# Attention scores from raw float32 tiles, with the 64-row tile first

## The chip, the cores and the metric

The kernel runs on one core of a Trainium2 chip, as one program. The core has five engines that each work through their own list of instructions in order: TensorE (PE in the profile, with its weight loads as PEld), VectorE (DVE), ScalarE (ACT), GpSimd (POOL) and SyncE (SP, which here issues every DMA). The metric is the device time of one execution in microseconds (us). Three runs of the kernel before took 1394.97, 1399.61 and 1401.06 us, median 1399.61.

## The reference

Attention with a computed position bias, and then two mixture layers:

```python
scores = scale * np.matmul(q, k.transpose(0, 1, 3, 2))      # 2 batches, 8 heads, 576 rows, 64 wide
x = (psi_rel / psi_i)[..., None]                            # 576 x 576 x 1
h = np.maximum(x @ w1 + b1, 0.0)                            # 32 hidden
bias = h @ w2                                               # one bias for each head, for both batches
scores = scores + bias.transpose(2, 0, 1)[None, :, :, :]
attn = np.exp(scores - np.max(scores, axis=-1, keepdims=True))
attn = attn / (np.sum(attn, axis=-1, keepdims=True) + 1e-09)
out = np.matmul(attn, v)
# then on the 1152 x 512 result: 4 experts (512-1024-512) weighted by given probabilities,
# then 8 experts (512-1024-512) weighted by a gate with 8 rounds of row and column scaling
```

Everything is float32.

## The kernel before

**Stages.** The attention comes first and takes about 200 us; the two mixture layers follow and take the rest. The change touches the attention alone.

**Bias groups.** The bias is made in 36 groups of 16 query rows. For a group DVE or ACT writes four hidden tiles (`emit_hid`), PE multiplies them by w2 in four quarter-height tiles (`emit_bias_mm`, tile `bps`), ACT copies the product out in two pieces into a staging tile (`emit_bias_out`, tile `bsts`), and SP writes that to a table in DRAM (`bd`, one for each row tile t = 0 to 4). The staging tile has three places, so the ACT copy of a group waits until the DMA of the group three before it has landed. A group's product takes a place of tag `sc` when it fills two banks, else the one place of tag `bps`. `load_bias` reads the table back as tile `bt` (two buffers): two DMAs for t < 4, four for t = 4.

**Units.** A unit is one pass over 128 query rows for a pair of heads: for t < 4 (t, head pair p, batch b), for t = 4 (the last 64 rows of both batches together) only (t, p). There are 36 units, numbered k = 0 to 35. `emit_S` computes the scores of both heads (tile `sc`, two places, both taken by one unit), `emit_max` adds the bias and takes the row maximum on DVE (tile `s`), `emit_exp` is ACT, `emit_T` transposes on PE two units later (tile `tp`; the tail and the reciprocals go into the scores' own banks while groups are left), `emit_evac` copies out (tile `at`), `emit_P` multiplies by V (tile `po`, one bank for all) three units later, and `emit_x` scales the product into `rows` on DVE. In each unit of the loop one more bias group is made (`groups(1)`), until all 36 are. From k = 16 to 18 and from 23 on, each unit also does one part of the preparation of the mixture layer (`pieces`, tiles `x10A`, `x10S`): ACT rounds, DVE or POOL subtracts.

**Scores before.** q and k are loaded raw (`qr`, `kr`); `prep_q` and `prep_k` split each into a rounded float32r tile and the float32r rest; `emit_S` adds three float32r products (rest x rounded, rounded x rest, rounded x rounded) in two column halves of 288, each for two heads that sit in the two 64-row halves of the array: 12 matmuls for t < 4, 24 for t = 4, where the zeros in q keep the batches apart.

**Order.** The order of every engine is the order in which the lines are written; nothing reorders it. SP's list too: a DMA that waits for a tile holds back all DMAs behind it.

Of the kernel before, what the change touches and what calls it, by code (L numbers as in the profile page):

```python
# [9 lines left out]
F32 = mybir.dt.float32  # L10
F32R = mybir.dt.float32r
AF = mybir.ActivationFunctionType
ALU = mybir.AluOpType
# [3 lines left out]
B, H, S, D = 2, 8, 576, 64  # L17
# [8 lines left out]
WARM = 10  # L26
# [22 lines left out]
def attn_moe_moe(ctx: ExitStack, tc: tile.TileContext, pack, keep, rel, qT, kT, vT, w, out):  # L49
# [12 lines left out]
    xa = pool("xa")  # L62
# [113 lines left out]
    def attention(moe):  # L176
# [26 lines left out]
        bdram = [dram.tile([H, (128 if t < 4 else 64) + 1, W], F32, name=f"bd{t}") for t in range(5)]  # L203


        tps_ = [(t, p) for t in (0, 4, 1, 2, 3) for p in range(4)]
        units = [(t, p, b) for t, p in tps_ for b in range(2 if t < 4 else 1)]
        U = len(units)
        kk, qq, bt, rawk, rawq = {}, {}, {}, {}, {}


        def load_k(p, b):
            i = 2 * p + b
            r = xa.tile([128, 1280], F32, tag=f"x0{XA[i % 4]}", name=f"kr{p}{b}")[:, 0:S]
            for h in range(2):
                sy.dma_start(out=r[64 * h:64 * h + 64], in_=kT[p, b, 0:64, S * h:S * h + S])
            rawk[p, b] = r

        def prep_k(p, b, hi):
            r = rawk.pop((p, b))  # L220
            kk[p, b] = ata.tile([128, 2, S], F32R, name=f"kk{p}{b}")
            h = kk[p, b][:, 0, :]
            if hi is sc:
                sc.activation(out=h, in_=r, func=AF.Copy)
            else:
                ve.tensor_copy(h, r)
            ve.tensor_tensor(out=kk[p, b][:, 1, :], in0=r, in1=h.bitcast(F32), op=ALU.subtract)

        def load_q(t, p):
            r = ata.tile([128, 256], F32, tag="qraw", name=f"qr{t}{p}", bufs=3)  # L230
            for h in range(2):
                sy.dma_start(
                    out=r[64 * h:64 * h + 64].rearrange("p (b c) -> p b c", b=2),
                    in_=qT[t, p, 0:64].rearrange("p (b h c) -> p h b c", b=2, h=2)[:, h],
                )
            rawq[t, p] = r

        def prep_q(t, p):
            r = rawq.pop((t, p))
            a = ata.tile([128, 2, 256], F32R, tag="qq", name=f"qq{t}{p}", bufs=3)  # L240
            ve.tensor_copy(a[:, 0, :], r)
            ve.tensor_tensor(out=a[:, 1, :], in0=r, in1=a[:, 0, :].bitcast(F32), op=ALU.subtract)
            qq[t, p] = a

        def load_bias(t, p):

# [21 lines left out]

        free = [(i, hids_[:, i * S:i * S + S]) for i in range(6)]
        taken = {}  # L270
        MORE = 56

        def emit_hid(g, eng, q):
            tt = 4 * g + q
# [62 lines left out]
        def emit_S(u):  # L337
            t, p, b = units[u]
            o = [ps.tile([128, 2, 512], F32, tag="sc", name=f"sc{u}{h}", bufs=2) for h in range(2)]

            todo = [(x, y, bb) for x, y in ((0, 1), (1, 0), (0, 0)) for bb in ([b] if t < 4 else [0, 1])]
            for j in range(2):
                for i, (x, y, bb) in enumerate(todo):
                    for h in range(2):
                        d = slice(64 * h, 64 * h + 64)
                        pe.matmul(  # L346
                            out=o[h][:, j, 0:288],
                            lhsT=qq[t, p][d, x, 128 * bb:128 * bb + 128],
                            rhs=kk[p, bb][d, y, 288 * j:288 * j + 288],
                            start=i == 0,  # L350
                            stop=i == len(todo) - 1,
                        )
# [98 lines left out]
        kq = [(p, b) for p in range(4) for b in range(2)]  # L451

        gp.memset(ones, 1.0)
        for _ in range(WARM):
            pe.matmul(out=po_all[:, 0, 0:128], lhsT=ones, rhs=ones, start=True, stop=True)
# [6 lines left out]
        load_q(*tps_[1])  # L462
        load_k(*kq[2])
        ve.tensor_scalar(b1psi, cst[:, C_PSI:C_PSI + 144], b1col, None, op0=ALU.mult)
        ve.tensor_scalar(w2n, cst[:, C_W2:C_W2 + 32], 8.0, None, op0=ALU.mult)
        ve.tensor_scalar(T, T, w1col, None, op0=ALU.mult)

        NGR = S // 16
        order = list(range(8)) + list(range(32, NGR)) + list(range(8, 32))
        made = 0  # L470
        started = 0

        def hids(k, engs=()):
            nonlocal started
            for i in range(k):
                if started < 4 * NGR and (free or started == 6):
                    emit_hid(order[started // 4], sc if i in engs else ve, started % 4)
                    started += 1
# [6 lines left out]
                    emit_bias_out(g, emit_bias_mm(g))  # L485
                    made += 1

        FIRST = 8
        hids(8, (1, 5))
        for g in range(FIRST):  # L490
            groups(1)
            if g == 0:
                prep_q(*tps_[0])
            if g == 1:
                prep_k(*kq[0], ve)
            hids(4, (1,))
            if g == 3:
                load_k(*kq[3])
            if g == 4:
                prep_k(*kq[1], ve)  # L500
            if g == 6:
                load_k(*kq[4])
                load_q(*tps_[2])

        load_bias(*tps_[0])
        load_bias(*tps_[1])
        load_k(*kq[5])
        load_q(*tps_[3])
        prep_q(*tps_[1])
        prep_k(*kq[2], sc)  # L510
        for _ in range(3):
            groups(1)
            hids(4)
        prep_k(*kq[3], sc)

        ti, work, first_split = 0, [], None
        for k in range(U + 3):
            first = False
            if k < U:
                t, p, b = units[k]  # L520
                first = b == 0
                if first:
                    ti = tps_.index((t, p))
                emit_S(k)
                emit_max(k)
                if k > 0:
                    emit_recip2(k - 1)
                if k >= 4:
                    emit_x(k - 4)
            elif k == U:  # L530
                emit_recip2(k - 1)
                emit_x(k - 4)
                st_sc.close()
                st_a.close()
                moe.open1()
                first_layer = moe.L1(0)
                for fn in first_layer[0:3]:
                    fn()
# [6 lines left out]
                emit_exp(k, 1)  # L545
            if k >= 2 and k - 2 < U:
                emit_evac(k - 2, 2, sc)
            groups(1)
            if k >= 2 and k - 2 < U:
                emit_evac(k - 2, 1, sc if made < NGR else ve)  # L550
            hids(2)
            if k < U:
                emit_recip(k)
            hids(2)
            if k >= 3 and k - 3 < U:
                emit_P(k - 3)
                if k >= U:
# [10 lines left out]
            if k < 4:  # L568
                prep_k(*kq[k + 4], sc)
# [409 lines left out]
```

## Time and profile before

The profiled execution took 1395.53 us; its span from the first to the last instruction is 1393.6 us, so 1.9 us lie around it. Its mean granted TensorE clock is 0.989.

| stretch (us) | what | PE busy | DVE busy | ACT busy | granted clock | DMA share |
|---|---|---|---|---|---|---|
| 0 to 26.26 | first bias groups | 21.21 | 21.33 | 18.62 | 1.00 | 0.66 |
| 26.26 to 56.03 | units 0 to 4 | 21.25 | 19.42 | 17.77 | 0.77 | 0.80 |
| 56.03 to 110.84 | units 5 to 15 | 51.53 | 38.98 | 41.74 | 1.00 | 0.69 |
| 110.84 to 149.03 | units 16 to 23 | 35.97 | 30.53 | 31.73 | 1.00 | 0.53 |
| 149.03 to 201.24 | units 24 to 35 | 43.46 | 40.65 | 38.99 | 1.00 | 0.40 |
| 201.24 to 1393.60 | mixture layers | 1170.51 | 651.80 | 357.81 | 0.99 | 0.13 |

A stretch starts where PE starts the scores of a unit. Busy time of PE is the union of matmuls that overlap, with modelled ends, so PE can be busy and not at its peak. A granted clock of 1.00 is 2.4 GHz and 0.50 is 1.2 GHz.

### The profile page before, as it was taken

The numbers are of one execution on the slowest core, as the hardware profiler recorded it, in microseconds if no ns is written. First come the engines' busy times: TensorE is split into PE (matmuls) and PEld (weight loads), VectorE is DVE, ScalarE is ACT, GpSimd is POOL, SyncE is SP. The second block draws the span as 40 slices with busy tenths as digits, with TensorE's granted clock in tenths as the row PEclk, the third lists the DMA queues.
The fourth block names the chain that finished last, engine by engine and source line by source line (L and its number), as shares of the span: only waits on it lengthen the run. The fifth ranks groups of instructions, "written<-read, shape, count | busy, mean of one in ns | idle before, by whom it ended". The sixth has DMA issues, their size and how long they took to land.

```text
span 1393.6 us, 22438 instructions
## 1 busy us (share of the span) xinstructions
PE 1343.9 (96%) x8763; PEld 1171.4 (84%) x8763; DVE 802.7 (58%) x1786; ACT 506.7 (36%) x1208; POOL 389.3 (28%) x391
## 2 busy tenths in 40 slices
PE   7899888999999999999989999999999999999998
PEld 3676677899898898888878898898998988988987
DVE  7768778464473563575584473564554644736543
ACT  6768764232241241343232241331331422413311
POOL 0111234053061260242151160250440622603400
PEclk9899999999999999999999999999999999999999
DMA  7765521011020020021021020020110200301110
GB/s 210 196 176 151 148 66 61 31 61 61 1 91 32 31 91 1 10 66 47 5 87 31 1 91 31 31 91 1 62 61 1 92 31 16 99 9 32 60 39 31
DMA packets 42169, 84.67 MB, mean 61 GB/s; under 512 B 10320, under 2 KB 17744, under 8 KB 42064
## 3 DMA queue, kind: packets, MB, share of 16 engines
q1 hardware_dynamic: 42064, 83.24, 19.7%
q8 instruction: 69, 1.13, 0.3%
q14 instruction: 36, 0.29, 0.1%
HBM read 69.97 MB, written 13.25 MB: 60 GB/s over the span
## 4 chain that ended last, share of the span: by engine, by line
PE 83%; DVE 9%; ACT 3%; DMA 2%; issue 1%; SPq 1%; DVEq 0%; ACTq 0%
PE y L726 41%; PE B L647 16%; PE C L647 10%; PE A L647 10%; DVE s L364 2%; PE po L435 2%; PE sc L346 1%; ACT s L377 1%; DMA bt<-bd 1%; PE bps L297 1%; PE tp L409 1%; ACT bsts L326 1%; DMA bd<-bsts 1%; DVE wt L157 0%; ACT at L418 0%
## 5 line engine op out<-in xcount | busy, mean ns | idle before, releaser
L726 PE MATMUL y<-gb,h 128*128 128x512 f32 x2592 | 717.8, 397 | 0.0
L726 PEld LDWEIGHTS y<-gb,h 128*128 128x128 f32 x2592 | 454.1, 189 | 57.2 <-issue 0.2
L162 POOL TENSOR_TENSOR gb<-rawb,gb 128x512 fp32r<-128x512 f32 x94 | 126.6, 1359 | 637.1 <-ACT gb L161 605.4
L658 ACT ACTIVATE h<-c 128x320 fp32r<-128x320 f32 (+1 forms) x288 | 119.2, 439 | 402.7 <-DVE c L655 401.5
L655 DVE TENSOR_TENSOR u<-B,s 128x320 f32<-128x320 f32 (+1 forms) x192 | 87.7, 457 | 307.9 <-PE B L647 307.9
L661 DVE SCALAR_TENSOR_TENSOR h<-c,h 128x320 fp32r<-128x320 f32 (+1 forms) x288 | 165.7, 592 | 49.1 <-ACT h L658 43.8
L655 DVE TENSOR_TENSOR c<-C,u 128x320 f32<-128x320 f32 (+1 forms) x192 | 87.6, 456 | 61.3 <-PE C L647 57.9
L162 POOL TENSOR_TENSOR ga<-rawa,ga 128x512 fp32r<-128x512 f32 x94 | 120.4, 1300 | 4.5 <-ACT ga L161 4.5
L162 POOL TENSOR_TENSOR ga<-wt,ga 128x512 fp32r<-128x512 f32 x94 | 104.6, 1132 | 47.7 <-ACT ga L161 27.5
L669 ACT ACTIVATE s<-A 128x320 f32<-128x320 f32 (+1 forms) x96 | 39.5, 411 | 181.3 <-PE A L647 181.2
L658 ACT ACTIVATE h<-A 128x320 fp32r<-128x320 f32 (+1 forms) x96 | 39.1, 408 | 151.0 <-PE A L647 150.5
L655 DVE TENSOR_TENSOR c<-B,s 128x320 f32<-128x320 f32 (+1 forms) x96 | 43.9, 458 | 81.6 <-PE B L647 80.3
L161 ACT ACTIVATE gb<-rawb 128x512 fp32r<-128x512 f32 x96 | 60.0, 626 | 67.6 <-DMA rawb<-in_w 67.6
L377 ACT ACTIVATE s<-s,stat 128x576 f32<-128x576 f32 x72 | 55.4, 769 | 41.5 <-DVE stat L364 40.7
L435 PEld LDWEIGHTS po<-at,V 128*64 128x64 f32 x800 | 39.4, 137 | 33.9 <-DVE rows L445 32.0
L647 PE MATMUL C<-x20S,ga 128*128 128x320 f32 x384 | 67.4, 311 | 0.0
L647 PE MATMUL A<-x20A,ga 128*128 128x320 f32 x384 | 67.1, 310 | 0.0
L647 PEld LDWEIGHTS C<-x20S,ga 128*128 128x128 f32 x384 | 62.1, 190 | 5.8
L647 PEld LDWEIGHTS A<-x20A,ga 128*128 128x128 f32 x384 | 62.0, 190 | 5.7
L647 PE MATMUL B<-x20S,ga 128*128 128x320 f32 x384 | 66.5, 308 | 0.0
L647 PEld LDWEIGHTS B<-x20S,ga 128*128 128x128 f32 x384 | 61.4, 188 | 5.7
L435 PE MATMUL po<-at,V 128*64 128x128 f32 (+1 forms) x800 | 47.7, 267 | 15.6 <-DVE rows L445 15.4
(163 smaller groups left out, 1917.0 us busy)
## 6 DMA issues: line engine op xcount, KB each, us to landing
rawa<-in_w SPq DMA_DIRECT2D x48, 512.0 KB, 4.0
rawb<-in_w SPq DMA_DIRECT2D x48, 512.0 KB, 4.9
bd<-bsts SPq DMA_DIRECT2D x36, 295.5 KB, 3.4
bt<-bd SPq DMA_DIRECT2D x16, 512.0 KB, 4.5
qr<-in_qT SPq DMA_DIRECT2D x40, 64.0 KB, 2.9
kr<-in_kT SPq DMA_DIRECT2D x16, 144.0 KB, 3.1
V<-in_vT SPq DMA_DIRECT2D x4, 512.0 KB, 4.6
bt<-bd SPq DMA_DIRECT2D x8, 256.0 KB, 4.1
```

The lines of the kernel that those rows point to most:

```text
L161: sc.activation(out=z(0), in_=src, func=AF.Copy)
L162: lo.tensor_tensor(out=z(1), in0=src, in1=z(0).bitcast(F32), op=ALU.subtract)
L297: pe.matmul(out=o[32 * q:32 * q + 32, j, 0:n], lhsT=w2n, rhs=hid[g, q][:, n * j:n * j + n], start=True, stop=True,)
L364: ve.tensor_tensor_reduce(out=s.rearrange("p (a j) -> p a j", a=2), in0=scps.pop((u, h))[:, :, 0:288], in1=bt[t, p][:, S * h:S * h + S].re ...
L377: sc.activation(out=s, in_=s, func=AF.Exp, scale=-1.0, bias=stat[u][:, h:h + 1], accum_out=stat[u][:, 2 + h:3 + h],)
L435: pe.matmul(out=o[64 * h:64 * h + 64, c0:c0 + n], lhsT=V[p][:, j, col:col + D], rhs=rhs, start=j == 0, stop=j == 4,)
L647: pe.matmul(out=ban[o], lhsT=a, rhs=x[:, z, k, :], start=not more and i == 0, stop=i == 5, skip_group_check=more,)
L655: ve.tensor_tensor(out=t[o], in0=ban[a], in1=t[b], op=ALU.add)
L658: sc.activation(out=h[f][:, 0, half, :], in_=src, func=AF.Relu)
L661: ve.scalar_tensor_tensor(out=h[f][:, 1, half, :], in0=src, scalar=0.0, in1=h[f][:, 0, half, :].bitcast(F32), op0=ALU.max, op1=ALU.subtract,)
L669: sc.activation(out=t["s1"], in_=ban["A"], func=AF.Copy)
L726: pe.matmul(out=self.y[t], lhsT=a, rhs=x, start=g == 0 and f == 0 and i == 0, stop=g == NP - 1 and f == 1 and i == 2,)
```

## The change

Four edits, all in the attention.

1. `emit_S` multiplies raw q by raw k as plain float32, one product in place of three: 4 matmuls for t < 4. For t = 4 each batch becomes a tile of 64 columns of the array, so 8 matmuls of 64 rows by 64 columns. `prep_q`, `prep_k` and the split tiles go; k is loaded straight into its tile, q into one of four buffers.
2. The order of the row tiles becomes 4, 0, 1, 2, 3 and that of the bias groups 32 to 35, then 0 to 31. Nine groups come before the loop in place of eleven; unit 4 makes two. In the first four units each unit now starts a new head pair, and k, V, q and the bias for the following ones are loaded in these units.
3. `emit_x(k - 4)` stands before `emit_S(k)` and `emit_max(k)` in place of behind them.
4. Six plain float32 matmuls of ones (`busy(6)`) follow the scores of units 0, 1 and 2.

```diff
-        tps_ = [(t, p) for t in (0, 4, 1, 2, 3) for p in range(4)]
+        tps_ = [(t, p) for t in (4, 0, 1, 2, 3) for p in range(4)]
...
         def load_k(p, b):
...
+            kk[p, b] = ata.tile([128, S], F32, name=f"kk{p}{b}")
             for h in range(2):
-                sy.dma_start(out=r[64 * h:64 * h + 64], in_=kT[p, b, 0:64, S * h:S * h + S])
-            rawk[p, b] = r
-
-        def prep_k(p, b, hi):
...
+                sy.dma_start(out=kk[p, b][64 * h:64 * h + 64], in_=kT[p, b, 0:64, S * h:S * h + S])
...
-        MORE = 56
+        MORE = 76
...
-            todo = [(x, y, bb) for x, y in ((0, 1), (1, 0), (0, 0)) for bb in ([b] if t < 4 else [0, 1])]
+            n = 128 if t < 4 else 64
             for j in range(2):
-                for i, (x, y, bb) in enumerate(todo):
+                for bb in [b] if t < 4 else [0, 1]:
+                    i = 0 if t < 4 else 64 * bb
                     for h in range(2):
                         d = slice(64 * h, 64 * h + 64)
                         pe.matmul(
-                            out=o[h][:, j, 0:288],
-                            lhsT=qq[t, p][d, x, 128 * bb:128 * bb + 128],
-                            rhs=kk[p, bb][d, y, 288 * j:288 * j + 288],
-                            start=i == 0,
-                            stop=i == len(todo) - 1,
+                            out=o[h][i:i + n, j, 0:288],
+                            lhsT=qq[t, p][d, 128 * bb + i:128 * bb + i + n],
+                            rhs=kk[p, bb][d, 288 * j:288 * j + 288],
+                            start=True,
+                            stop=True,
                         )
...
-        order = list(range(8)) + list(range(32, NGR)) + list(range(8, 32))
+        order = list(range(32, NGR)) + list(range(32))
...
-        FIRST = 8
+        FIRST = 4
...
+        load_q(*tps_[1])
+        load_k(*kq[2])
+        load_k(*kq[3])
         load_bias(*tps_[0])
         load_bias(*tps_[1])
...
+        load_v(0)
+        for g in range(5):
             groups(1)
-            hids(4)
+            hids(4, (1,))
...
+                if k >= 4:
+                    emit_x(k - 4)
                 emit_S(k)
+                if k < 3:
+                    busy(6)
                 emit_max(k)
                 if k > 0:
                     emit_recip2(k - 1)
-                if k >= 4:
-                    emit_x(k - 4)
...
-            groups(1)
+            groups(2 if k == 4 else 1)
...
             if first:
                 if ti + 2 < len(tps_):
-                    prep_q(*tps_[ti + 2])
-                if ti + 4 < len(tps_):
-                    load_q(*tps_[ti + 4])
+                    load_q(*tps_[ti + 2])
...
             if k < 2:
-                load_k(*kq[k + 6])
-            if k < 8 and k % 2 == 0:
-                load_v(k // 2)
+                load_k(*kq[2 * k + 4])
+                load_k(*kq[2 * k + 5])
+            if k < 3:
+                load_v(k + 1)
```

SP, the DMAs ahead of the first units; before (kr and qr are raw k and q, bd the table in DRAM, bt the bias read back, the digits are row tile or head pair):

```order
L216 DMA kr10_137<-in_kT 64x576 x2
L329 DMA bd0_104<-bsts_110 16x8x591 x4
L216 DMA kr11_224<-in_kT 64x576 x2
L329 DMA bd0_104<-bsts_110 16x8x591 x3
L216 DMA kr20_266<-in_kT 64x576 x2
L232 DMA qr02_269<-in_qT 64x2x128 x2
L329 DMA bd0_104<-bsts_110 16x8x591
L255 DMA bt00_284<-bd0_104 128x2x512
L256 DMA bt00_284<-bd0_104 128x2x64
L255 DMA bt01_287<-bd0_104 128x2x512
L256 DMA bt01_287<-bd0_104 128x2x64
```

SP, the same place in the changed kernel (kk is k, V0 the values of head pair 0):

```order
L215 DMA kk11_218<-in_kT 64x576 x2
L235 DMA bt40_221<-bd4_108 64x2x512
L236 DMA bt40_221<-bd4_108 64x2x64
L235 DMA bt40_221<-bd4_108 64x2x512
L236 DMA bt40_221<-bd4_108 64x2x64
L235 DMA bt41_226<-bd4_108 64x2x512
L236 DMA bt41_226<-bd4_108 64x2x64
L235 DMA bt41_226<-bd4_108 64x2x512
L236 DMA bt41_226<-bd4_108 64x2x64
L197 DMA V0_100<-in_vT 128x4x256
L201 DMA V0_100<-in_vT 64x2x64 x2
L309 DMA bd0_104<-bsts_110 16x8x591 x6
```

Six writes of groups to DRAM now stand behind the eight bias reads and the three DMAs of V.

DVE, a unit in the middle of the attention, before (s and stat are the maximum, rows is emit_x, hids the next group's hidden tiles):

```order
L364 ISA s6_748,stat6_747<-sc60_731,bt03_580 128x576
L364 ISA stat6_747 128x1
L364 ISA s6_748,stat6_747<-sc61_732,bt03_580 128x576
L364 ISA stat6_747 128x1
L387 RECIPROCAL stat5_677<-stat5_677 128x2
L445 TENSOR_TENSOR rows0_76<-po_95,at22_624 128x128
L283 TENSOR_SCALAR hids_109<-T_99,b1psi_98 128x352 x2
```

DVE, a unit of the changed kernel:

```order
L426 TENSOR_TENSOR rows0_76<-po_95,at42_744 128x128
L345 ISA s8_854,stat8_853<-sc80_845,bt02_711 128x576
L345 ISA stat8_853 128x1
L345 ISA s8_854,stat8_853<-sc81_846,bt02_711 128x576
L345 ISA stat8_853 128x1
L368 RECIPROCAL stat7_793<-stat7_793 128x2
L263 TENSOR_SCALAR hids_109<-T_99,b1psi_98 128x320 x4
```

The product of unit k - 4 is read ahead of the maximum of unit k, in place of behind it and its reciprocal.

## Rows read from the trace of the kernel before

**Rows 1.** Timeline of PE, scores of units and the first mixture matmul (start, duration).
```profile
26.26 1.05 PE L346 MATMUL sc<-kk,qq 64*128 64x288 f32 x11 [0.81 <-ACT bsts L326]
...
56.03 1.34 PE L346 MATMUL sc<-kk,qq 64*128 64x288 f32 x12
...
69.14 1.93 PE L346 MATMUL sc<-kk,qq 64*128 64x288 f32 x24
...
97.78 1.27 PE L346 MATMUL sc<-kk,qq 64*128 64x288 f32 x12
...
106.53 1.13 PE L346 MATMUL sc<-kk,qq 64*128 64x288 f32 x12
...
110.84 1.14 PE L346 MATMUL sc<-kk,qq 64*128 64x288 f32 x12
...
149.03 1.06 PE L346 MATMUL sc<-kk,qq 64*128 64x288 f32 x12
...
201.24 1.15 PE L647 MATMUL A<-x10A,ga 128*128 128x320 f32 x6
```

**Rows 2.** Waits of DVE at 50 to 150 us (total us, times, longest).
```profile
DVE s L364 <- DMA bt<-bd: 7.0, 3, 2.7
```

**Rows 3.** Waits of PE at 150 to 200 us.
```profile
PE po L435 <- DVE rows L445: 8.7, 11, 1.5
```

**Rows 4.** Stretch of the half clock (length, busy PE, PEld, DVE, ACT, POOL, clock, DMA).
```profile
28.86:39.10 10.24, 6.86 (x42) 3.33 (x44) 6.82 (x20) 4.99 (x12) 1.42 (x4) 0.50 0.72 206
```

**Rows 5.** Timeline of PE, plain float32 bias products of two widths.
```profile
89.42 0.72 PE L297 MATMUL bps<-hids,w2n 128*32 128x304 f32 x8
...
151.26 1.07 PE L297 MATMUL bps<-hids,w2n 128*32 128x512 f32 x8
```

**Rows 6.** Timeline of SP, issues (start, time on SP's queue).
```profile
8.77 5.59 SPq L329 DMA_DIRECT2D bd<-bsts  x4
14.41 1.24 SPq L216 DMA_DIRECT2D kr<-in_kT  x2
...
20.26 1.23 SPq L232 DMA_DIRECT2D qr<-in_qT  x2
...
24.90 0.39 SPq L255 DMA_DIRECT2D bt<-bd  x1
...
39.17 0.58 SPq L197 DMA_DIRECT2D V<-in_vT  x1
39.85 1.20 SPq L201 DMA_DIRECT2D V<-in_vT  x2
41.15 0.55 SPq L329 DMA_DIRECT2D bd<-bsts  x1
...
62.14 0.60 SPq L255 DMA_DIRECT2D bt<-bd  x1
```

**Rows 7.** Page, DMA issues: KB each, median us from issue to landing.
```profile
bd<-bsts SPq DMA_DIRECT2D x36, 295.5 KB, 3.4
bt<-bd SPq DMA_DIRECT2D x16, 512.0 KB, 4.5
...
kr<-in_kT SPq DMA_DIRECT2D x16, 144.0 KB, 3.1
```

**Rows 8.** Timeline of ACT, first exponential and a group copied out after it.
```profile
29.79 0.78 ACT L377 ACTIVATE s<-s,stat 128x576 f32<-128x576 f32 x1 [3.00 <-DVE stat L364]
...
33.82 1.05 ACT L326 ACTIVATE bsts<-bps,cst 128x16 f32<-128x16 f32 x2 [2.40 <-DMA bd<-bsts]
```

**Rows 9.** Timeline of DVE, a late unit.
```profile
158.97 0.29 DVE L100 TENSOR_TENSOR x10S<-t,x10S 128x128 fp32r<-128x128 f32 x1 [1.16 <-ACT x10S L99]
...
161.04 0.27 DVE L445 TENSOR_TENSOR rows<-po,at 128x128 f32<-128x128 f32 x1
```

**Rows 10.** Groups of DVE by line at 0 to 400 us (busy us, mean ns).
```profile
L242 DVE TENSOR_TENSOR qq<-qr,qq 128x256 fp32r<-128x256 f32 x20 | 8.5, 425 | 0.7
L227 DVE TENSOR_TENSOR kk<-kr,kk 128x576 fp32r<-128x576 f32 x8 | 6.1, 758 | 9.9 <-ACT kk L224 8.1 <-DMA kr<-in_kT 1.7
```

More of the change, by code (lines that the diff above doesn't have):

```diff
@@ L203, in attention @@
         bdram = [dram.tile([H, (128 if t < 4 else 64) + 1, W], F32, name=f"bd{t}") for t in range(5)]
-        tps_ = [(t, p) for t in (0, 4, 1, 2, 3) for p in range(4)]
+        tps_ = [(t, p) for t in (4, 0, 1, 2, 3) for p in range(4)]
         units = [(t, p, b) for t, p in tps_ for b in range(2 if t < 4 else 1)]
         U = len(units)
-        kk, qq, bt, rawk, rawq = {}, {}, {}, {}, {}
+        kk, qq, bt = {}, {}, {}
         def load_k(p, b):
-            i = 2 * p + b
-            r = xa.tile([128, 1280], F32, tag=f"x0{XA[i % 4]}", name=f"kr{p}{b}")[:, 0:S]
+            kk[p, b] = ata.tile([128, S], F32, name=f"kk{p}{b}")
             for h in range(2):
-                sy.dma_start(out=r[64 * h:64 * h + 64], in_=kT[p, b, 0:64, S * h:S * h + S])
-            rawk[p, b] = r
-        def prep_k(p, b, hi):
[L220 to L227, printed above, removed]
+                sy.dma_start(out=kk[p, b][64 * h:64 * h + 64], in_=kT[p, b, 0:64, S * h:S * h + S])
         def load_q(t, p):
-            r = ata.tile([128, 256], F32, tag="qraw", name=f"qr{t}{p}", bufs=3)
+            qq[t, p] = ata.tile([128, 256], F32, tag="qq", name=f"qq{t}{p}", bufs=4)
             for h in range(2):
                 sy.dma_start(
-                    out=r[64 * h:64 * h + 64].rearrange("p (b c) -> p b c", b=2),
+                    out=qq[t, p][64 * h:64 * h + 64].rearrange("p (b c) -> p b c", b=2),
                     in_=qT[t, p, 0:64].rearrange("p (b h c) -> p h b c", b=2, h=2)[:, h],
                 )
[L236 to L243, printed above, removed]
         def load_bias(t, p):
@@ L453, in attention, with busy @@
         gp.memset(ones, 1.0)
-        for _ in range(WARM):
-            pe.matmul(out=po_all[:, 0, 0:128], lhsT=ones, rhs=ones, start=True, stop=True)
+        def busy(n):
+            for _ in range(n):
+                pe.matmul(out=po_all[:, 0, 0:128], lhsT=ones, rhs=ones, start=True, stop=True)
+        busy(WARM)
         sy.dma_start(out=cst, in_=pack)
@@ L461, in attention @@
         sy.dma_start(out=kept, in_=keep)
-        load_q(*tps_[1])
-        load_k(*kq[2])
         ve.tensor_scalar(b1psi, cst[:, C_PSI:C_PSI + 144], b1col, None, op0=ALU.mult)
@@ L491, in attention @@
             groups(1)
[L492 to L495, printed above, removed]
             hids(4, (1,))
[L497 to L503, printed above, removed]
+        load_q(*tps_[1])
+        load_k(*kq[2])
+        load_k(*kq[3])
         load_bias(*tps_[0])
         load_bias(*tps_[1])
[L507 to L511, printed above, removed]
+        load_v(0)
+        for g in range(5):
             groups(1)
-            hids(4)
-        prep_k(*kq[3], sc)
+            hids(4, (1,))
         ti, work, first_split = 0, [], None
@@ L553, in attention @@
                 emit_recip(k)
-            hids(2)
+            hids(6 if k == 3 else 2)
             if k >= 3 and k - 3 < U:
@@ L567, in attention @@
                 load_bias(*tps_[ti + 2])
-            if k < 4:
-                prep_k(*kq[k + 4], sc)
             if k < 2:
-                load_k(*kq[k + 6])
-            if k < 8 and k % 2 == 0:
-                load_v(k // 2)
+                load_k(*kq[2 * k + 4])
+                load_k(*kq[2 * k + 5])
+            if k < 3:
+                load_v(k + 1)
             if k == 8:
```

## The prediction

> **What bounds the kernel now.** I read the table of stretches first. The mixture layers, from 201.24 us on, keep PE busy nearly throughout, and no line of theirs changes; what the change is worth must come out of the first 201.24 us. There I went along PE's timeline from one start of scores to the next [rows 1]. Units 5 to 15 take 110.84 - 56.03 = 54.81 us for eleven, 4.98 each, but the dense ones take 110.84 - 106.53 = 4.31. The difference sits in one place: from 69.14 (the first unit of the 64-row tile) to 97.78 five units take 28.64 us, 7.1 more than five dense ones. The waits of DVE name the cause: the maximum waits 7.0 us in three waits for the bias read back [rows 2]. A unit of that tile comes one to a head pair, so its four bias DMAs have half as long to land.
>
> At 150 to 200 us PE waits 8.7 us for `emit_x` [rows 3]: the product's bank is read on DVE behind the maximum, which waits for the scores. In the first 56 us neither PE nor DVE nor ACT is full; there I looked at SP's issues and their landings [rows 6, 7] and at what ACT waits for [rows 8].
>
> **Scores.** No row shows a plain float32 matmul in 64-row halves. The nearest is the bias product, plain float32 in four quarter-height tiles: 304 columns take 0.72 us and 512 take 1.07 [rows 5], so 0.35 / 208 = 1.68 ns a column plus 0.21 fixed. The four run together: in turn each column would cost 0.42 ns, less than in float32r, where six full-height products of 320 columns take 1.15 us at 201.24 [rows 1], 0.49 ns a column without the fixed part. And float32r runs two 64-row halves together: twelve scores matmuls of 288 columns take 1.06 at 149.03 [rows 1], where twelve in turn would take about 2 by those products. If plain float32 in halves overlaps too, a unit's scores are 2 x 288 x 1.68 ns + 0.21 = 1.18 us, 0.12 more than now. If the halves take turns, it is 4 x 0.484 + 0.21 = 2.15, 1.09 more. The best is no fixed part, 0.97, 0.09 less than now. I take 1.18, because both kinds of tiles in the trace overlap. For the 64-row tile four tiles together give 1.18, pairs 2.15, against 1.93 now at 69.14 [rows 1]; these units will wait for loads, so this counts nothing.
>
> The scores stand in the loop that sets a dense unit: scores, half of the maximum, two exponentials with two evacuations, and the next scores need the bank that the last of these frees. PE itself is as full. So 0.12 is paid for each dense unit: 4.43.
>
> **Splits that go.** On DVE 6.1 us for k and 8.5 for the rests of q [rows 10], with their copies. In the dense units DVE waits for PE's scores anyway, so I count nothing; in the first units their cover is ACT and SP, which stay late.
>
> **The start.** SP issues in order. From its rows [rows 6]: a k tile 1.25 us, q 1.25, V 1.9 with gaps, a group's write 0.6, one bias DMA 0.39 to 0.60, so four with gaps 1.7 to 2.6; I take 2.2. The fourth group left SP at 8.77 + 5.59 = 14.4; without the splits between them on DVE I put it at 13.6. Then SP holds q, two k tiles, eight bias reads and V: 13.6 + 1.25 + 2.5 + 4.4 + 1.9 = 23.65. Only then comes the write of the fifth group. It lands 3.4 us after issue at the median [rows 7]; with the bias and V bytes ahead of it I take 3.8: 27.45. The eighth group needs that group's staging place, as ACT does now at 33.82, where it waits 2.40 us for such a landing [rows 8]. Its copy takes 1.05: 28.5. The first scores need the banks that this copy frees, so they start at 28.5 against 26.26, although two groups fewer come first.
>
> By then PE has had nothing for some 9 us; in the trace a stretch of gaps like this stands at the half clock, 1.2 GHz, for 10.24 us [rows 4]. So the first scores take 2.2 (the 0.97 doubled, and the fixed part), the first half of the maximum 0.9, two exponentials 0.78 each [rows 8]: 33.2. Six fill matmuls of 128 columns are 6 x 0.215 = 1.3 us at full clock and 2.6 at half. They stand ahead of the tenth group's product, which leaves ACT at about 35.3. Now SP: its write, q, four bias reads, two k tiles end at 35.3 + 0.6 + 1.25 + 2.2 + 2.5 = 41.85, and k lands 3.1 after its last issue [rows 7] at 44.4: unit 2. V, a write, q, four reads, two k tiles: 41.85 + 1.9 + 0.6 + 1.25 + 2.2 + 2.5 = 50.3, landed 52.8: unit 3. V and a write at 52.2; the bias of unit 4 needs that write landed (55.6) and then 4.5 us [rows 7]: 60.1. From the maximum to the next scores a dense unit takes 4.31 - 1.06 = 3.25, so unit 5 starts at 63.4, against 56.03: **+7.4**. The fills don't change this: between them PE waits 6 to 8 us for loads.
>
> Here the Trainium skill speaks the other way ("DMA: Bandwidth & Descriptors", Issuing engines are not separate DMA queues): the sequencer's time to start a DMA "is usually small relative to the DMA itself". By the rows 47 DMAs of about 0.6 us are 28 us of SP in the 37 from 13.6 to 50.3, and a landing is 3 to 4.5; the rule's result is the first rival below.
>
> **The rest.** Units 5 to 15 have no 64-row tile any more, and a bias read has three units to land: 11 x 4.43 = 48.7 in place of 54.81, **-6.1**. Units 16 to 23: five or six dense ones of eight pay 0.12, **+0.7**. In units 24 to 35 two of three run at the pace of a chain that starts at the maximum, goes through ACT's evacuations and rounding and ends in DVE's subtraction (its wait of 1.16 for ACT [rows 9]) ahead of the next maximum. The moved `emit_x`, 0.27 long [rows 9], of which I count 0.2, now stands between that subtraction and the maximum. So the 8.7 us of PE's wait are not a gain: where it goes, this chain is late next, 8 x 0.2 = 1.6 dearer, and only the third without rounding gains some 0.4, 4 x 0.3 with the longer scores: **+0.3**.
>
> Sum: 7.4 - 6.1 + 0.7 + 0.3 = +2.3. On the profiled execution, 1395.53 with 1.9 around its span, that is 1397.8. That execution lies 4.1 below the median of the runs; on the median 1399.61 it is 1402. What waited for the 64-row tile's loads in the middle waits for them at the start. Within 0.5% is 7.0 us, about what a measurement tells from no change.
>
> **Rivals.** *A lean start*: issues cost little and only landings count. Then the first bias read lands at about 22.5, unit 0's scores run at 22, five units at 4.43 to 5 put unit 5 at 44 to 47. -10.5 - 6.1 + 1 gives 1384; half of it, with unit 5 near 52, gives 1391. For it: DMA share is 0.80, not 1, at units 0 to 4. Against: SP's rows, which are the same instructions. Taken at 1386.
> *A longer start*: bias DMAs at 0.60 each (+0.4 a unit's four, four times), landings 0.7 longer, fills at half clock: unit 5 near 68, +7; and the bias of row tiles 1, 2 and 3 is now read in the very unit that makes its last group, so SP waits there for 3.4 us each time. With 1 us lost at each, 1410.
> *Halves in turn* (slower): plain float32 in 64-row halves does not overlap. Each of 32 units pays 1.09 in place of 0.12: 32 x 0.97 = 31, 1433. For it: no row shows the pair; against: both parts of it. It decides from 0.15 us a unit more than I take (scores of 1.33): 32 x 0.15 = 4.7, which with +2.3 is 7.
>
> **Numbers.** My forecast 0.56 (1402, its own range 1393 to 1409), lean start 0.17, longer start 0.17, halves in turn 0.10. Range 1389 to 1412: it leaves out the halves, the lower half of the lean start and the end of the longer one, 0.2 in all. Faster by over 0.5%: 0.16 of the lean start and 0.04 of mine, 0.20. Slower: 0.10 + 0.11 + 0.03 = 0.24. Between: 0.56.
>
> **What would show it.** In the changed profile: unit 0's scores near 28.5, with ACT waiting for a landed write before the eighth group's copy; units 2 and 3 waiting for k; unit 5 at 63; a half clock between 25 and 50; scores rows of 1.18; 4.43 from unit to unit in 5 to 15; PE's wait for `emit_x` gone at 150 to 200 us, and the first mixture matmul at 203 all the same. Unit 5 before 56, or scores of 2.15, would make the prediction wrong.

## The result and the profile after

The changed kernel takes 1412.38 us (median of four runs, 1408.82 to 1413.96) against 1397.92 us for the kernel before in the same runs (four, 1394.97 to 1401.06). The ratio is 1.0100, 95% interval 1.0074 to 1.0125: slower by 1%. The forecast was no change (1402), and the time lies at the very end of the stated range (1389 to 1412). What happened is nearest to the rival called the longer start (1410), for more reasons than that rival named.

The profiled execution took 1413.96 us, span 1412.2. Its timeline of PE, start and duration of a unit's scores in us (compare with [rows 1]):

```profile
31.78 2.19 PE L327 MATMUL sc<-kk,qq 64*64 64x288 f32 x14 [10.99 <-ACT bsts L306]
...
37.98 1.20 PE L327 MATMUL sc<-kk,qq 64*64 64x288 f32 x16
...
47.38 4.51 PE L327 MATMUL sc<-kk,qq 64*64 64x288 f32 x16 [5.73 <-DMA kk<-in_kT]
...
60.03 1.18 PE L327 MATMUL sc<-kk,qq 64*64 64x288 f32 x10 [0.63 <-DMA kk<-in_kT]
...
64.59 1.24 PE L327 MATMUL sc<-kk,qq 64*128 64x288 f32 x8
...
76.85 1.93 PE L327 MATMUL sc<-kk,qq 64*128 64x288 f32 x8
...
82.08 1.27 PE L327 MATMUL sc<-kk,qq 64*128 64x288 f32 x8
...
165.99 1.24 PE L327 MATMUL sc<-kk,qq 64*128 64x288 f32 x8
...
217.95 1.15 PE L617 MATMUL A<-x10A,ga 128*128 128x320 f32 x6
```

These are units 0 to 6, unit 24 and the first mixture matmul; of unit 3 the row shows the part after a wait, its scores had begun at 57.6. By stages, against [rows 1] (units 16 start at 110.84 and 126.7):

| stage | before | after | difference | forecast |
|---|---|---|---|---|
| to the start of unit 5 | 56.03 | 76.85 | +20.8 | +7.4 |
| units 5 to 15 | 54.8 | 49.8 | -5.0 | -6.1 |
| units 16 to 23 | 38.2 | 39.3 | +1.1 | +0.7 |
| units 24 to 35 | 52.2 | 52.0 | -0.2 | +0.3 |
| mixture layers | 1192.4 | 1194.2 | +1.8 | 0 |

The profiled execution of before lies 2.4 us below the median of its runs and that of after 1.6 above, so this table sums to 18.5 where the medians differ by 14.5. The start alone makes the kernel slower. SP's timeline shows how it begins (start, time on the queue; compare with [rows 6]):

```profile
8.66 5.31 SPq L309 DMA_DIRECT2D bd<-bsts  x4
14.02 1.98 SPq L220 DMA_DIRECT2D qq<-in_qT  x2
16.04 2.52 SPq L215 DMA_DIRECT2D kk<-in_kT  x4
18.66 0.61 SPq L235 DMA_DIRECT2D bt<-bd  x1
...
23.86 0.59 SPq L197 DMA_DIRECT2D V<-in_vT  x1
24.55 1.19 SPq L201 DMA_DIRECT2D V<-in_vT  x2
25.85 13.92 SPq L309 DMA_DIRECT2D bd<-bsts  x6
...
63.11 0.37 SPq L235 DMA_DIRECT2D bt<-bd  x1
```

Eight bias reads of 0.60 or 0.61 stand between 18.66 and 23.8. ACT meanwhile waits for the fifth group's landing, and the copies and fills that follow are these (timeline of ACT, then of PE; compare with [rows 8]):

```profile
30.68 1.05 ACT L306 ACTIVATE bsts<-bps,cst 128x528 f32<-128x528 f32 x2 [11.62 <-DMA bd<-bsts]
...
38.18 1.05 ACT L306 ACTIVATE bsts<-bps,cst 128x496 f32<-128x496 f32 x2 [1.73 <-PE bps L277]
```

```profile
33.90 2.93 PE L438 MATMUL po<-ones 128*128 128x128 f32 x12
...
39.11 1.60 PE L438 MATMUL po<-ones 128*128 128x128 f32 x12
...
52.30 2.50 PE L438 MATMUL po<-ones 128*128 128x128 f32 x12
...
72.97 1.62 PE L277 MATMUL bps<-hidS,w2n 128*32 128x416 f32 x8 [5.03 <-ACT bsts L306]
74.52 2.40 PE L416 MATMUL po<-at,V 128*64 128x64 f32 x40
```

The last two rows are the second bias group of unit 4 and what is queued behind it. Three stretches of the start stand near the half clock, 30.8 us together; [rows 4] shows the longest of before, 10.24 us (length, busy time of PE, PEld, DVE, ACT and POOL, granted clock, DMA share, GB/s):

```profile
23.30:37.00 13.70, 5.22 (x30) 3.62 (x34) 2.93 (x8) 4.74 (x10) 0.47 (x1) 0.51 0.71 195
43.80:54.10 10.30, 6.71 (x27) 3.89 (x28) 2.31 (x8) 0.87 (x2) 0.43 (x1) 0.52 0.85 217
71.10:77.90 6.80, 4.93 (x52) 3.26 (x54) 0.79 (x3) 3.29 (x8) 0.21 (x1) 0.53 0.43 111
```

### The profile page after: what moved, and what is told of

Same layout as the page of the kernel before. It is cut to its first block, busy times and chain, and to the rows that moved or that the text cites. A ratio compares the mean times of both kernels' runs of the same rounds, so it can differ in the third digit from the quotient of the medians.

```text
span 1412.2 us, 22199 instructions
## 1 busy us (share of the span) xinstructions
PE 1359.2 (96%) x8639; PEld 1172.6 (83%) x8639; DVE 780.5 (55%) x1734; ACT 505.2 (36%) x1204; POOL 387.3 (27%) x391
## 4 chain that ended last, share of the span: by engine, by line
PE 84%; DVE 7%; ACT 4%; DMA 2%; SPq 2%; issue 1%; POOL 0%; DVEq 0%; ACTq 0%; POOLq 0%
PE y L696 41%; PE B L617 15%; PE C L617 10%; PE A L617 10%; PE po L416 2%; PE sc L327 2%; ACT s L358 1%; PE bps L277 1%; PE tp L390 1%; ACT at L399 1%; ACT bsts L306 1%; DVE s L345 1%; PE po L438 1%; DMA V<-in_vT 1%; SPq L215 1%
## 5 line engine op out<-in xcount | busy, mean ns | idle before, releaser
L161 ACT ACTIVATE gb<-rawb 128x512 fp32r<-128x512 f32 x96 | 60.1, 627 | 69.2 <-DMA rawb<-in_w 69.2
L345 DVE CUSTOM_DVE_ANT_0 s<-sc,bt 128x576 f32<-128x576 f32 x72 | 51.7, 753 | 48.6 <-PE sc L327 29.4
L327 PE MATMUL sc<-kk,qq 64*128 64x288 f32 (+1 forms) x320 | 55.5, 459 | 21.0 <-ACT bsts L306 11.0
```

What stands on the lines that cost most here:

```text
L161: sc.activation(out=z(0), in_=src, func=AF.Copy)
L327: pe.matmul(out=o[h][i:i + n, j, 0:288], lhsT=qq[t, p][d, 128 * bb + i:128 * bb + i + n], rhs=kk[p, bb][d, 288 * j:288 * j + 288], start=True,
L345: ve.tensor_tensor_reduce(out=s.rearrange("p (a j) -> p a j", a=2), in0=scps.pop((u, h))[:, :, 0:288], in1=bt[t, p][:, S * h:S * h + S].re ...
```

## The experiments

The theory: the start is late because SP issues in order, so that group writes and loads stand behind bias reads, k and V; the scores and emit_x cost next to nothing, the fills nothing. The rivals: the scores' own price, landings and bytes in place of issues, the fills, and the second group of unit 4.

All positions are starts on PE's timeline, in us, read from one profiled execution of each kernel. The mixture layers differ by up to 10 us between profiled executions, so a stage is compared by its positions, the whole by the medians (of 4 to 10 executions) and the ratio to the kernel before in the same runs. Positions also differ a little before an edit acts: unit 0's scores go on at 31.78 in the changed kernel, at 30.98 in a_g8 and 30.88 in a_nofill, which are the same up to there. One position that differs by 1 us tells nothing.

| run | unit 1 | unit 3 | unit 6 | unit 16 | mixture | median | ratio (95%) |
|---|---|---|---|---|---|---|---|
| before | 31.9 | 42.1 | 60.6 | 110.8 | 201.2 | 1397.92 | |
| changed | 38.0 | 57.6 | 82.1 | 126.7 | 217.9 | 1412.38 | 1.0100 (1.0074, 1.0125) |
| e_raw | 31.8 | 42.2 | 57.0 | 108.8 | 200.9 | 1397.66 | 1.0000 (0.9990, 1.0009) |
| e_x | 31.9 | 42.4 | 61.1 | 111.4 | 200.8 | 1398.42 | 1.0002 (0.9988, 1.0017) |
| a_g8 | 37.2 | 56.9 | 78.5 | 126.0 | 217.0 | 1409.79 | 1.0092 (1.0069, 1.0115) |
| a_pool | 33.4 | 51.1 | 73.3 | 117.9 | 209.2 | 1405.38 | 1.0047 (1.0030, 1.0065) |
| a_late | 32.2 | 51.4 | 73.5 | 118.0 | 209.2 | 1405.88 | 1.0061 (1.0038, 1.0085) |
| a_latepool | 30.8 | 49.7 | 72.2 | 116.8 | 208.0 | 1404.97 | 1.0052 (1.0031, 1.0074) |
| a_nofill | 34.8 | 54.0 | 75.1 | 119.7 | 210.9 | 1407.76 | 1.0073 (1.0044, 1.0101) |
| a_bt4 | 29.9 | 52.1 | 74.4 | 119.0 | 210.2 | 1408.69 | 1.0078 (1.0064, 1.0092) |
| a_bt4_v0 | 30.1 | 51.0 | 73.5 | 118.1 | 209.3 | 1408.11 | 1.0074 (1.0057, 1.0091) |
| b_bt3 | 32.0 | 42.8 | 61.1 | 107.3 | 197.7 | 1393.80 | 0.9971 (0.9948, 0.9994) |
| raw_bt3 | 32.1 | 43.0 | 57.9 | 102.8 | 195.0 | 1390.78 | 0.9947 (0.9925, 0.9969) |
| raw_bt3_pool | 32.6 | 42.1 | 56.8 | 101.8 | 194.0 | 1390.38 | 0.9947 (0.9934, 0.9959) |

**One edit alone, on the kernel before.** e_raw has the scores of the change, with k loaded straight into its tile, and everything else at its old place:

```diff
-        prep_q(*tps_[1])
-        prep_k(*kq[2], sc)
...
-            todo = [(x, y, bb) for x, y in ((0, 1), (1, 0), (0, 0)) for bb in ([b] if t < 4 else [0, 1])]
+            n = 128 if t < 4 else 64
...
+                            out=o[h][i:i + n, j, 0:288],
```

> The kernel before with the raw float32 scores alone: no splits of q and k, the 64-row tile as 64-column tiles, but the tile order, the eleven first groups, the place of emit_x and SP's order as before, and no fills. Theory (the slowdown is the start in the new order): unit 5 starts at 54 to 56 us, no later than before (56.03); the wait of the 64-row tile in units 8 to 12 stays (units 5 to 15 in 54 to 56 us); scores rows 1.24 against 1.06, so units 16 to 35 some 0.1 to 0.2 us each dearer, +2 to +4; the whole 0 to +4 us against before. Rival (the scores themselves cost the 14.5 us): +10 us or more, spread evenly over the units.

No change in the whole. Unit 6 comes 3.6 us earlier than before, which I put down to the splits that go, though no run takes them out alone; units 24 to 35 take 53.4 in place of 52.2 and units 16 to 23 38.7 in place of 38.2, with scores of 1.24 for 1.06. Units 5 to 15 took 56.4, a little above the forecast. In the old order the scores don't cost the 14.5 us.

e_x moves one call:

```diff
+                if k >= 4:
+                    emit_x(k - 4)
                 emit_S(k)
```

> The kernel before with emit_x moved ahead of the scores and nothing else. Theory (as in the prediction): PE's 8.7 us of waits for emit_x at 150 to 200 us go, and another wait takes their place; first mixture matmul within 1 us of 201.2, the whole within 2 us. Rival one (the waits were real cost): units 24 to 35 some 5 to 8 us shorter. Rival two (it delays DVE's maximum everywhere): +0.2 us in each of 32 units, +6.

The whole is unchanged. The waits of PE over the last twelve units, against 8.7 [rows 3]:

```profile
PE tl L397 <- ACT at L418: 5.7, 8, 0.7
PE po L435 <- DVE rows L445: 0.7, 3, 0.4
```

The wait for `emit_x` went and one for ACT's evacuation took its place, as the theory said; units 24 to 35 take 50.6 for 52.2, a gain of 1.6 where the prediction had 1.6 dearer in eight units and as much cheaper in the other four. With e_raw's +1.2 that is -0.4, near the -0.2 of the changed kernel: the two parts nearly cancel.

**The second group of unit 4.** a_g8:

```diff
-            groups(2 if k == 4 else 1)
+            groups(2 if k == 8 else 1)
...
-            hids(6 if k == 3 else 2)
+            hids(6 if k == 7 else 2)
```

> The changed kernel with the unit that makes two bias groups put at unit 8 in place of unit 4 (and its four more hidden tiles at unit 7). Theory (PE's 5.03 us wait for the copy of the first of the two groups in unit 4 was itself 5 us of the late unit 5): unit 5 at 71 to 73 in place of 76.85, unit 16 at 121 to 124 if the double group costs less in unit 8, where nothing waits for a bias; the whole -3 to -5 against the changed kernel. Rival (unit 5 is late for its bias or k, and the double group only stands in that time): unit 5 at 76 to 77, the whole unchanged within 1.

Unit 5 begins 8.5 earlier, but its own scores then wait for the late evacuations; at unit 6 3.6 us are left, of which 0.8 were there at unit 1 already, and unit 8 takes 7.47 with the second group in place of 4.51 without it, which gives 3.0 back. Unit 16 is 0.7 earlier, no more than unit 1. Neither text is right: the second group costs some 3 us in either unit, and the start of unit 5 overstates the late start by its place.

**SP's order and SP's load.** a_pool changes the issuing queue of k and V, and a_late the order on SP with nothing taken off it:

```diff
-                sy.dma_start(out=kk[p, b][64 * h:64 * h + 64], in_=kT[p, b, 0:64, S * h:S * h + S])
+                gp.dma_start(out=kk[p, b][64 * h:64 * h + 64], in_=kT[p, b, 0:64, S * h:S * h + S])
```

> The changed kernel with the loads of k and V issued by POOL at the same places, not by SP; q, bias reads and group writes stay on SP. Theory (SP's issues, some 0.6 us for a DMA, set the start): the fifth group's write leaves SP some 4.4 us earlier (two k tiles 2.5, V 1.9), so ACT's wait of 11.62 for its landing falls to 7 to 8, unit 0's second half of the scores starts at 27 to 29, units 2 and 3 no longer wait for k (42 to 45, 49 to 53), unit 5 at 64 to 70, the whole -6 to -12 against the changed kernel. Rival (landings and bytes on the wire set it, issues are cheap): same stage times within 2 us.

```diff
-        load_q(*tps_[1])
-        load_k(*kq[2])
-        load_k(*kq[3])
-        load_bias(*tps_[0])
-        load_bias(*tps_[1])
-        load_v(0)
         for g in range(5):
             groups(1)
             hids(4, (1,))
+        load_bias(*tps_[0])
+        load_q(*tps_[1])
+        load_bias(*tps_[1])
+        load_k(*kq[2])
+        load_k(*kq[3])
+        load_v(0)
```

> The changed kernel with the loads that stand between the fourth and the fifth group (q, two k tiles, eight bias reads, V) put behind the ninth group, the first four bias reads first. Nothing is taken off SP. Theory (each write waits for what SP holds ahead of it, and the places are in order): ACT's wait of 11.6 us for the fifth group's landing goes, PE's half clock before unit 0 too, the ninth group is copied out by 22 to 24, the first bias lands at 29 to 31, unit 1 starts at 32 to 35 in place of 38.0. But the k tiles of units 2 and 3 and V now come last, so of these 4 us no more than half is left at unit 6 (80 to 82 in place of 82.1), the whole -0 to -4 against the changed kernel. Rival (the wait for the one landing was the whole loss): unit 6 at 70 to 73, the whole -10.

With k and V on POOL, ACT's wait is 7.45 in place of 11.62 (timeline of ACT):

```profile
27.00 1.05 ACT L306 ACTIVATE bsts<-bps,cst 128x528 f32<-128x528 f32 x2 [7.45 <-DMA bd<-bsts]
```

That is the 4.2 us of issues that were taken out of the way; unit 0 goes on at 28.1, unit 5 starts at 68.5, unit 6 8.7 earlier, all as expected. Unit 2 now waits for q in place of k. With SP's order alone changed, the ninth group leaves SP at 20.95 and the first maximum starts at 27.75, where it was 34.01 (timeline of a_late):

```profile
20.95 0.52 SPq L309 DMA_DIRECT2D bd<-bsts  x1
...
27.75 0.76 DVE L345 CUSTOM_DVE_ANT_0 s<-sc,bt 128x576 f32<-128x576 f32 x1 [8.81 <-DMA bt<-bd]
```

Unit 6 comes 8.6 earlier. Here my theory fell: it allowed two, and the rival (the wait for the one landing is the loss) is nearly met. SP's total load is not what set the start; what stood ahead of one group's write was. (In a_late the half clock also lasts 24.0 us of the start in place of 30.8; that share was not parted from the order's.) a_latepool has both edits:

> Both: the loads behind the ninth group, and k and V issued by POOL. Theory (SP's queue): k and V no longer stand in front of anything, so units 0 to 3 come at the pace of bias reads and landings: unit 1 at 32 to 35, unit 3 at 43 to 48, unit 6 at 66 to 71 (73.3 with POOL alone), the whole 3 to 7 us below POOL alone (1405). Rival (what is left with POOL alone is landings of the groups that unit 4 needs): unit 6 within 1.5 us of 73.

Unit 6 comes 1.2 before that of a_late and 1.1 before that of a_pool, so again the rival: with the order mended, k and V on another queue are worth little, no more than one position can tell. SP now waits for ACT in 38.9 of the first 82 us.

**The fills.** a_nofill:

```diff
-                if k < 3:
-                    busy(6)
```

> The changed kernel without the fill matmuls in the first three units. Theory (they stand in PE's waits): stages within 1 us of the changed kernel, unit 6 at 81 to 83. Rival one (they stand in the way of the bias product behind them): 1 to 2 us shorter a unit, unit 6 at 77 to 79. Rival two (they keep the clock up): the half clock lasts longer than the 13.65, 10.24 and 6.83 us of now, unit 6 at 84 or later.

Unit 6 comes 7.0 earlier in the profiled execution, against the theory and beyond rival one; the median is 4.6 lower, with intervals that overlap. The three fills of the changed kernel last 2.93 + 1.60 + 2.50 = 7.03, two of them at the half clock. That this is the same number is chance; the 7.0 are made of other pieces. The first 0.9 are no fill's: ACT's copy of the eighth group, ahead of them all, starts at 29.78 in place of 30.68. The copy behind the first fill comes next (timeline of ACT):

```profile
35.45 1.03 ACT L306 ACTIVATE bsts<-bps,cst 128x496 f32<-128x496 f32 x2
```

It starts 2.7 earlier than at 38.18. SP's write of that group, and q, bias and k behind it, follow: q is issued at 37.07 in place of 39.82. From there SP is busy nearly throughout up to the write of the twelfth group, whose landing the bias of unit 4 waits for; it is issued at 55.31 in place of 58.87, and the bias is read at 58.98 in place of 63.11. The other two fills held up nothing on SP: in the changed kernel the copies of the eleventh and twelfth group were done 5.5 and 1.0 us before SP came to their writes. The maximum of unit 4, which waited for the bias, now waits for the scores alone and starts 4.6 earlier (timeline of DVE, changed kernel, then a_nofill):

```profile
68.74 0.76 DVE L345 CUSTOM_DVE_ANT_0 s<-sc,bt 128x576 f32<-128x576 f32 x1 [3.32 <-DMA bt<-bd]
```

```profile
64.18 0.76 DVE L345 CUSTOM_DVE_ANT_0 s<-sc,bt 128x576 f32<-128x576 f32 x1 [0.79 <-PE sc L327]
```

The last 2.4 are the clock's. From the second group's product to unit 6 the changed kernel takes 9.1 us, more than half of it in the half clock from 71.1; a_nofill takes 6.7, at the full clock by then (length, busy times, clock and DMA as above, a window of a_nofill):

```profile
71.10:77.90 6.80, 6.80 (x89) 4.66 (x87) 4.64 (x16) 4.44 (x10) 0.54 (x2) 1.00 0.37 86
```

In sum its half clock is no shorter, 30.65 us (from 23.2, 40.2 and 57.3) against 30.8, so rival two is out as well: without the fills the half clock lies elsewhere, but lasts as long.

**What is left of the start.** a_bt4 adds to a_latepool two bias places and reads all four head pairs of the 64-row tile ahead of the loop; a_bt4_v0 then leaves the loads of three of the four V tiles out:

```diff
-            x = ata.tile([128, 2 * 640], F32, tag="bt", name=f"bt{t}{p}", bufs=2)
+            x = ata.tile([128, 2 * 640], F32, tag="bt", name=f"bt{t}{p}", bufs=4)
...
-                load_v(k + 1)
+                V[k + 1] = V[0]
```

> The kernel of a_latepool (changed kernel, loads behind the ninth group, k and V from POOL) with four bias places in place of two: all four bias reads of the 64-row tile stand ahead of the loop, later ones are read as early as their groups allow. Theory (what is left of the start is that each 64-row unit's bias goes through the same two places, issued, landed and used one after the other): units 1 to 3 no longer wait for a bias, unit 4 starts at 46 to 52 in place of 56.3, unit 6 at 62 to 67 in place of 72.2, the whole -5 to -10 against a_latepool. Rival (k, q or the three groups that unit 4 still needs set the pace): unit 6 at 71 to 73.

> The kernel of a_bt4 without the loads of V for the second to fourth head pair: the first V is used for all (so the attention of the others is not the reference's). 1.73 MB of loads go, 9 DMAs, none of them SP's; at the 220 GB/s of the crowded stretches that is 7.9 us of the DMA engines. Theory (with issue and places out of the way the bytes of four head pairs in four units are the bound: DMA share 1.06 and 1.07 at 32 to 44 us, q 8.6 us late behind the reads): unit 2 starts at 41 to 43 in place of 45.1, unit 6 at 67 to 71 in place of 74.4. Rival (the queue of twelve bias reads ahead of q on SP, whatever the other loads): unit 2 at 44.5 to 45.5, unit 6 at 73 to 75.

The places are not it: unit 6 at 74.4, 2.2 later. Unit 2 now waits for a 64 KB load of q, and the DMA engines are full (timeline of PE, and two windows of a_bt4):

```profile
45.16 3.12 PE L327 MATMUL sc<-kk,qq 64*64 64x288 f32 x16 [8.63 <-DMA qq<-in_qT]
```

```profile
32.00:38.00 6.00, 4.53 (x27) 2.79 (x20) 3.50 (x9) 3.02 (x8) 5.50 (x12) 0.71 1.06 218
38.00:44.00 6.00, 0.00 (x0) 0.00 (x0) 0.00 (x0) 0.00 (x0) 3.16 (x7) 0.57 1.07 298
```

Without those V loads unit 2 came at 43.5 and unit 6 at 73.5, 1.7 and 0.9 earlier, where the theory had 2 to 4 and 3 to 7. Unit 6 is as the rival said, unit 2 lies between the two, and the engines stay at a share of 1.05 from 32 to 44 us without V, so this doesn't rule the bytes out. In both the bias of unit 4 still follows a group that is made in unit 2. What holds the start near 72 to 74 is open: the bytes of the bias reads, the order behind them and that last group were not tried apart, nor was a_late without fills.

**A third bias place in the old order.** b_bt3 changes the kernel before, and raw_bt3 adds the raw scores; raw_bt3_pool issues k and V from POOL:

```diff
-            x = ata.tile([128, 2 * 640], F32, tag="bt", name=f"bt{t}{p}", bufs=2)
+            x = ata.tile([128, 2 * 640], F32, tag="bt", name=f"bt{t}{p}", bufs=3)
...
-            if k < U and last and ti + 2 < len(tps_):
-                load_bias(*tps_[ti + 2])
+            while k < U and last and nbias < min(ti + (3 if k > 1 else 2) + 1, len(tps_)) and made >= need(tps_[nbias][0]):
+                load_bias(*tps_[nbias])
+                nbias += 1
```

Here `need(t)` is the count of groups that the table of row tile t takes.

> The kernel before, with three places for the bias tile in place of two, and each read issued one head pair earlier once it can be. Theory (the 64-row tile in the middle loses its time by the short lead of its bias reads, not by its place or its products): units 8 to 12 in 22 to 24 us in place of 28.6, units 5 to 15 in 48 to 50 in place of 54.8, start unchanged (unit 5 at 55 to 57), the whole -5 to -7 against before: the gain that the new order had in the middle, without its start. Rival (SP's time for four reads a unit bounds it, whatever the lead): units 5 to 15 at 53 or more, the whole within 2.

> The kernel before with the raw float32 scores and with the third bias place. Theory: unit 5 at 52 to 53 (as with the scores alone, 52.4), units 5 to 15 in 49 to 51, the later units 0.1 to 0.2 dearer each: the whole -4 to -8 against before, within 2 of the third place alone. Rival (raw scores cost 0.2 in each unit without anything in return): 3 to 5 us above the third place alone.

> The kernel of raw_bt3 (before, with raw float32 scores and a third bias place) with k and V issued by POOL. Theory (SP's queue holds the first units up there too, though less): unit 5 at 48 to 52 in place of 53.2, the rest as in raw_bt3, the whole 1 to 5 us below it, 1386 to 1390. Rival (the order of before has its loads early enough): within 1 us of raw_bt3.

In b_bt3 DVE's wait for the bias at 50 to 150 us is one of 1.1 us, where [rows 2] had 7.0:

```profile
DVE s L364 <- DMA bt<-bd: 1.1, 1, 1.1
```

Units 5 to 15 take 50.7, 4.1 less, and the whole is 0.3% faster (limits 0.1 and 0.5), a little short of the forecast: the four 64-row units still take 5.0 to 5.1 with scores of 1.9 to 2.0. In raw_bt3 their scores are four 64-column tiles at a time and take 1.2 to 1.5 (timeline of PE in b_bt3, then raw_bt3), and the units 4.3 to 4.6:

```profile
79.85 1.97 PE L346 MATMUL sc<-kk,qq 64*128 64x288 f32 x24
```

```profile
80.15 1.47 PE L327 MATMUL sc<-kk,qq 64*64 64x288 f32 x16
```

The first mixture matmul stands at 195.0, 6.2 before that of the kernel before, and the ratio is 0.9947 (0.9925 to 0.9969): faster than the kernel before, and so than the changed one. The median is 3.0 below that of the third place alone, where I had said within 2, but the intervals of the two overlap. POOL's queue adds 1.0 there and 0.4 in the median, as its rival said; it is the same kernel within what can be told.

## Where the prediction was right and where it was wrong

**The range, and luck.** The measured 1412.4 lies at the very end of the stated range, which reached to 1412 to take in the longer start (1410). The forecast's own sum, +2.3 and 1402, failed: +14.5 was measured, and its own range ended at 1409. That the stated range reaches the result is luck: the second group of unit 4 was in no term and no rival, and the forecast called the fills free.

**The bound was read rightly.** Only the attention moved (the mixture's +1.8 is within what it differs by itself), and the wait for the 64-row tile's bias in the middle went (-5.0 for -6.1). A unit takes 4.46 us on average from 82.08 to 126.7, for the forecast 4.43, and its scores 1.24 to 1.43 for 1.18, far from 2.15: the halves overlap, so "halves in turn" is out. Among DVE's waits from 76 to 166 us there is none for a bias, where [rows 2] had 7.0. The extra 1.1 of the middle is mostly unit 5, which took 5.23.

**The failed step is the start's sum.** It had +7.4 us up to unit 5, and +20.8 was measured. Its chain was the right one, but each link was too cheap and one was missing; by the prediction's own points:

| step | forecast | measured | grown by |
|---|---|---|---|
| last of four writes off SP | 13.6 | 13.97 | +0.4 |
| fifth group's write issued | 23.65 | 25.85 | +1.8 |
| scores of unit 0 go on | 28.5 | 31.78 | +1.1 |
| tenth group's copy done | 35.3 | 39.2 | +0.6 |
| bias of unit 4 read | 55.6 | 63.11 | +3.6 |
| landed | 60.1 | 68.74 | +1.1 |
| unit 5 | 63.4 | 76.85 | +4.8 |

The second row is SP: eight bias reads with their gaps were 5.2 in place of 4.4, and q 1.98 in place of 1.25. The text had 1.7 to 2.6 for four reads and took 2.2; 2.6 was right, and of its rows [rows 6] the one of the 64-row tile itself, at 62.14, had the 0.60 that came. The third row is the landing: the write issued at 25.85 released ACT at 30.68, after 4.8 in place of 3.8, though the median landing is 3.3, no longer than in [rows 7] (the page's DMA issues, KB each, median us from issue to landing):

```profile
bd<-bsts SPq DMA_DIRECT2D x36, 295.5 KB, 3.3
```

From 20 to 60 us alone the median of the changed kernel is 4.5. The median of the whole kernel was no measure for the one landing that stands behind the crowd.

**The fills were called free.** The prediction counted the first ahead of the tenth group's product and said of all three that they change nothing, "between them PE waits 6 to 8 us for loads". But k, q and bias stand on SP behind the write of the tenth group, whose product the first fill delays, so there the wait does not hide the fill, it starts later. Unit 6 is 21.5 late (82.1 for 60.6), and without the fills 7.0 less (a_nofill, 0.9 of it before any fill), by way of that write and of a half clock that then doesn't fall on unit 4's second group. The other two fills did stand in waits, as the prediction said of all three. Nor did they hold the clock: after the one at 39.11, at full speed, the next stretch stands at 0.52 from 43.8.

**The second group of unit 4 was not in the sum.** The change names it, and the working never priced it. Its product needs the one `bps` place, which the first group's copy frees; that copy stands in ACT's order behind unit 4's exponentials, and the product of unit 1 with V and the next scores stand behind it in PE's. Its 3 us (a_g8) and the half clock from 71.1 (1.7 up to unit 5, by a_nofill) make the +4.8 of the table's last line.

**The splits were counted at nothing.** With them gone from the old order, together with the longer scores, unit 6 came 3.6 earlier (e_raw). If the changed kernel has this gain too, its order, second group and fills cost that much more than the 21.5.

**Issues against landings.** The prediction set its sum against a rule of the Trainium skill ("DMA: Bandwidth & Descriptors", Issuing engines are not separate DMA queues): to start a DMA usually takes little time beside the DMA itself, and issuing from several engines saves no more than that. DMA by DMA the trace agrees: a bias read holds SP for 0.60 and lands after 4.3 at the median. The lean start is out all the same: unit 5 came at 76.85 for 44 to 52. Yet my own reading, that SP's sum of issues sets the start, went too far the other way: a_late kept all issues on SP and got 8.6 us back by order alone. What cost was one write behind 11.9 us of other issues (13.97 to 25.85) while ACT waited for that write to land. With that order mended, issuing k and V from a second queue was worth 1.2; without, it was worth 8.7. The rule of the Trainium skill fits the 1.2, and says nothing of what waits behind the issues, which made the 8.7.

**The longer start** said unit 5 near 68 by dearer reads, later landings and fills at the half clock, and these three did come. Its other part, reads of row tiles 1 to 3 that wait in the unit of their last group, came on SP (the read behind the write issued at 101.04 left at 104.50) but cost nothing: no unit from 6 to 18 takes more than 4.57, and DVE waits for no bias up to 218 us.

**emit_x and the late units.** PE's wait for it is 0.6 in place of 8.7 [rows 3], and the pace did not move (waits of PE in the changed kernel's last twelve units, total us, times, longest):

```profile
PE tl L378 <- ACT at L399: 3.0, 7, 0.6
...
PE po L416 <- DVE rows L426: 0.6, 2, 0.4
```

The chain named as late next is there: DVE's waits for ACT's rounding in the same units, of which one was 1.16 in [rows 9], are up to 2.6 now, 6.7 where they were 4.0 in four before:

```profile
DVE x10S L100 <- ACT x10S L99: 6.7, 4, 2.6
```

The sum nearly came out (+0.3, by its own terms 1.6 - 1.2 = 0.4, against -0.2), and that is luck: e_x gained 1.6 there, where the prediction had its gains and losses cancel, and e_raw lost 1.2, where it counted 0.1 in each of four units.

**Where the 16.7 us at the mixture's start are.** The scores and emit_x are -0.3 and -0.4. So the order of the tiles with its loads, the second group and the fills make the rest, by what is left over: a_late gives back 8.7 and a_nofill 7.0, each alone (that they add up was not shown).

## What to carry to other kernels

A wait hides a piece of work only if what ends the wait is not itself issued behind that work: follow the loads on their queue back to the instruction that releases them. On an in-order queue, look for the one transfer that another engine waits for and see what is queued ahead of it, before adding the issues up. A stall from short lead can be mended by one more buffer where it stands; here that gave, with the raw scores, 0.5%, and the change that moved the stalled tile to the front, where loads crowd, and put fills there lost 1%.

## What the runs showed of the hardware

Plain float32 products run four 64-row by 64-column tiles together: 16 records of 288 columns take 1.20 us where 8 records of 64 rows by 128 columns take 1.24, at the full clock. At the half clock 14 records of the former take 2.19.

A small load can land late among large ones: q, 64 KB, lands after 3.1 us at the median of the changed kernel (3.7 from 20 to 60 us), and after 6.6 in a_bt4 from 20 to 60 us, with V and k from POOL and sixteen bias reads around it.
